# Copying the first transposed x tiles out of PSUM in smaller pieces, on two engines, with one warm-up matmul fewer

## The chip, the cores and the metric

The kernel runs on one core of one Trainium2 chip. The metric is the device time of one execution in microseconds (us). The times come with a profile of one execution, whose "span" is some 2 us shorter than the time. TensorE does the matmuls, VectorE and ScalarE copy and compute, GpSimd masks, and SyncE and ScalarE issue the DMAs of this stage. In the profile lines they are PE (with PEld for weight loads), DVE, ACT, POOL and SP.

## The reference, cut to what matters

```python
x = A_x                                             # 2048 x 512, bf16
g = _sigmoid((x * gate_w).sum(-1, keepdims=True))
a = _A_ref(x, ...)      # 4 segments of 512 tokens: causal attention of 32 heads plus a running memory, then @ wo
b = _B_ref(x, ...)      # (gelu(x @ w_gate) * (x @ w_up)) @ w_down
return g * a + (1 - g) * b
```

Every projection needs x with its features on the partitions, that is, transposed. The change touches only how the first segment of x gets there, in the first seven microseconds.

## The kernel before

The kernel is a fixed list of tasks for each engine (`ORDER`). An emitter works out the semaphore waits from the regions that the tasks read and write. The first segment of x is loaded untransposed in two halves of 256 tokens (u = 0, 1). TensorE transposes each half in 128 x 128 blocks into PSUM, and copies bring it to `xT[0]`. The other segments come through transposing DMAs.

```python
    for i in range(12):                                   # warm-ups ("fillers"): the product is never read
        gw = Grp(banks)
        n = 384 if i in (6, 9) else 512
        task(f"warm{i}", PE, [... e.matmul(gw.f32()[:, 0:n], ones[:, 0:128], ones[:, 0:n], ...)])
    XB = XALL.bitcast(BF)
    for u in range(2):                                    # half of the tokens
        for i in range(2):                                # two of the four feature blocks
            src = XB[:, 1024 * (2 * u + i):1024 * (2 * u + i) + 512]...      # one PSUM bank each
            key = ("X", 2 * u + i)
            task(f"x0t{i}_{u}", PE, [... e.transpose(...) for k in range(2) for a in range(2)])   # 4 transposes
            S.add(Task(f"x0ev{i}_{u}", {ACT: ..., DVE: [... e.tensor_copy(dst, src) ...]}))       # 512 columns
```

The heads of the orders; `K0_t.j` is matmul j of K tile t in the first segment. K matmuls 0 and 1 need feature blocks 0 and 1 of the first tokens, K matmuls 2 and 3 need blocks 2 and 3.

```python
"pe":  "warm0 ... warm9 x0t0_0 x0t1_0 warm10 warm11 K0_0.0 K0_1.0 K0_2.0 K0_3.0 K0_0.1 ... x0t0_1 x0t1_1 K0_0.2 ..."
"dve": "x0ev0_0 x0ev1_0 x0ev0_1 K0_1ev ..."
"act": "w_wk0 w_wk1 w_wq0 w_wq1 tload x0ev1_1 K0_0even ..."
```

The softmax here doesn't subtract the row's maximum and nothing guards it: scores larger than these inputs give would overflow.

## Time and profile before

| | before |
|---|---|
| time, median of the first 3 runs | 268.13 us (267.79 to 268.9) |
| span of the profiled execution | 265.8 us |
| TensorE busy | 261.9 us, 99% |
| first transpose, first K matmul (start) | 4.49, 5.40 us |

How to read it: TensorE is busy end to end, so anything that only shortens another engine's work cannot show. The stage to look at is the head. The distance from the first transpose to the first K matmul is the measure used throughout, because it does not contain the moment at which x arrives.

### The profile page before, as it was taken

What the parts mean: (1) busy time and instruction counts of PE and PEld (TensorE: products, weight loads), DVE (VectorE), ACT (ScalarE), POOL (GpSimd) and SP (SyncE); (2) the same over time, 40 slices, a digit from 0 to 9 for tenths busy, and PEclk for the clock granted to TensorE, in tenths of its full rate; (3) what the DMA queues carried; (4) which work ended last, traced back from release to release, by engine and by line L of the source; (5) the groups of instructions that cost most, each with busy time, mean ns of one, the idle gap of its engine ahead of it and who ended that gap; (6) DMA issues with size and microseconds to landing.
All of it is one profiled execution on the core that took longest, in us unless ns stands there. A gap on an engine that the chain in (4) does not pass through costs nothing.

```text
span 265.8 us, 7150 instructions
## 1 busy us (share of the span) xinstructions
PE 261.9 (99%) x3022; PEld 118.9 (45%) x3022; DVE 198.1 (75%) x389; ACT 210.1 (79%) x186; POOL 105.5 (40%) x256
## 2 busy tenths in 40 slices
PE   8999999999999999999999999999999999999995
PEld 4644354444444435444444444443444444343452
DVE  1798869988988588986767968898685847694651
ACT  2699998999998898898967888867876886767712
POOL 8204777453101358173830162354173071436310
PEclk9999999999999999999999999999999999999999
DMA  6952323518520433200001333200000031300102
GB/s 219 334 162 42 63 81 71 151 40 295 151 76 0 99 66 80 80 0 2 2 0 23 97 83 77 86 2 22 2 2 0 2 75 31 78 25 0 42 0 79
DMA packets 32751, 18.22 MB, mean 69 GB/s; under 512 B 20560, under 2 KB 32720, under 8 KB 32720
## 3 DMA queue, kind: packets, MB, share of 16 engines
q1 hardware_dynamic: 31632, 16.73, 23.5%
q10 hardware_dynamic: 1088, 1.05, 1.1%
q8 instruction: 23, 0.38, 0.6%
q14 instruction: 8, 0.07, 0.1%
HBM read 9.84 MB, written 2.10 MB: 45 GB/s over the span
## 4 chain that ended last, share of the span: by engine, by line
PE 98%; ACT 1%; issue 0%; ACTq 0%
PE psW L498 76%; PE psXALL L859 9%; PE psW L909 6%; PE psXALL L498 3%; PE psW L583 2%; PE psW L917 1%; PE psW L825 1%; ACT pt L866 1%; PE psXALL L591 0%; ACT ost L1038 0%; ACTq L394 0%
## 5 line engine op out<-in xcount | busy, mean ns | idle before, releaser
L866 ACT ACTIVATE pt<-psXALL 128x2048 bf16<-128x2048 f32 x64 | 120.1, 1877 | 25.2 <-PE psXALL L859 20.1
L870 POOL TENSOR_SCALAR_AFFINE_SELECT pt<-pt 128x256 bf16<-128x256 bf16 x128 | 57.3, 456 | 106.4 <-ACT pt L866 101.8
L498 PE MATMUL psW<-xT,wu 128*128 128x512 bf16 x224 | 56.3, 380 | 0.0
L498 PE MATMUL psW<-xT,wg 128*128 128x512 bf16 x224 | 54.2, 380 | 0.0
L498 PE MATMUL psW<-wd,hT 128*128 128x512 bf16 x210 | 53.5, 380 | 0.0
L1009 DVE TENSOR_TENSOR hT<-psW,hT 128x512 bf16<-128x512 f32 x56 | 37.2, 685 | 18.6 <-PE psW L498 18.2
L870 POOL TENSOR_SCALAR_AFFINE_SELECT ptl<-ptl 128x512 bf16<-128x512 bf16 x32 | 23.0, 720 | 33.4 <-ACT ptl L866 31.8
L924 DVE STREAM_TRANSPOSE tb<-psW 128x512 f32<-128x512 f32 x32 | 21.5, 699 | 14.0 <-PE psW L917 14.0
L498 PEld LDWEIGHTS psW<-xT,wg 128*128 128x128 bf16 x224 | 20.4, 98 | 24.3 <-issue 1.5
L498 PEld LDWEIGHTS psW<-xT,wu 128*128 128x128 bf16 x224 | 20.2, 98 | 24.4 <-issue 2.7
L498 PEld LDWEIGHTS psW<-wd,hT 128*128 128x128 bf16 x210 | 19.2, 98 | 22.8 <-issue 2.1
L859 PE MATMUL psXALL<-qT,kpad 32*128 32x320 bf16 (+3 forms) x512 | 25.4, 273 | 0.2 <-ACT pt L866 0.2
L993 ACT ACTIVATE hT<-psW 128x512 bf16<-128x512 f32 x28 | 15.4, 599 | 8.0 <-PE psW L498 8.0
L859 PEld LDWEIGHTS psXALL<-qT,kpad 32*128 32x128 bf16 x512 | 7.6, 92 | 25.8 <-ACT pt L866 16.1
L909 PE MATMUL psW<-pt,vaug 128*17 128x192 bf16 (+3 forms) x512 | 18.8, 273 | 0.0
L866 ACT ACTIVATE ptl<-psXALL 128x2048 bf16<-128x2048 f32 x8 | 15.0, 1877 | 3.7 <-PE psXALL L859 3.7
L498 PE MATMUL psW<-xT,wk 128*128 128x512 bf16 (+1 forms) x80 | 17.8, 337 | 0.0
L498 PE MATMUL psW<-wv,xT 128*128 128x512 bf16 x64 | 17.3, 381 | 0.0
L498 PE MATMUL psW<-wo,oT 128*128 128x512 bf16 x60 | 16.4, 380 | 0.0
L768 POOL COPY exsT<-exs 32x4 f32<-32x4 f32 x64 | 13.4, 210 | 7.2 <-ACT exs L759 3.5
L909 PEld LDWEIGHTS psW<-pt,vaug 128*17 128x17 bf16 x512 | 10.2, 90 | 8.8 <-issue 2.8
L498 PE MATMUL psW<-xT,wq 128*128 128x512 bf16 x48 | 12.8, 380 | 0.0
(101 smaller groups left out, 308.0 us busy)
## 6 DMA issues: line engine op xcount, KB each, us to landing
out_dram<-ost SPq DMA_DIRECT2D x15, 128.0 KB, 1.7
wg<-in_B_w_gate_dram SPq DMA_DIRECT2D x2, 896.0 KB, 6.8
wu<-in_B_w_up_dram SPq DMA_DIRECT2D x2, 896.0 KB, 6.0
wd<-in_B_w_down_dram SPq DMA_DIRECT2D x2, 896.0 KB, 5.8
phkt<-in_A_x_dram SPq DMA_DIRECT2D x3, 512.0 KB, 4.3
vlow<-vaug SPq DMA_DIRECT2D x8, 136.0 KB, 2.7
wk<-in_A_wk_dram ACTq DMA_DIRECT2D x2, 256.0 KB, 4.4
hT<-in_A_x_dram SPq DMA_DIRECT2D x2, 256.0 KB, 4.0
```

The costliest lines, as they stand in the source:

```text
L498: return Instr(lambda e: e.matmul(view(), lhsT, rhs, start=first, stop=last), reads=reads, writes=[fkey if fkey is not None else g.key], e ...
L583: task(f"warm{i}", PE, [Instr(lambda e, gw=gw, n=n: e.matmul(gw.f32()[:, 0:n], ones[:, 0:128], ones[:, 0:n], start=True, stop=True), [], [ ...
L768: cross = task(f"exsT{s}", POOL, [Instr(lambda e, g=g, c=c: e.tensor_copy(exsT[sl][32 * g:32 * g + 32, c:16:4], exs[32 * c:32 * c + 32, s4 ...
L825: Instr(lambda e, t=t, kt=kt, c=c: e.matmul(gm.f32()[32 * c:32 * c + 32, 34 * t:34 * t + 34].rearrange("p (j e) -> p j e", e=17), phkt[:, ...
L859: instrs.append(Instr(lambda e, g=g, lhs=lhs, rhs=rhs, c0=c0, ncol=ncol: e.matmul(X[g][:, c0:c0 + ncol], lhs(32 * g), rhs(32 * g), start=T ...
L866: prev_exp[0] = exp_task(s, f"exp{s}_{t}{name}", [Instr(lambda e: e.activation(dst[:], XALL[:, :].rearrange("p (g c) -> p g c", g=4), ACTF ...
L870: task(f"msk{s}_{t}{name}", POOL, [Instr(lambda e, view=view, pat=pat, base=base: e.affine_select(out=view, in_=view, compare_op=ALU.is_ge ...
L909: instrs.append(Instr(lambda e, t=t, q=q, kb=kb, slot=slot, c0=c0: e.matmul(gp.f32()[32 * q:32 * q + 17, 128 * kb + 64:512], Vaug[sl][:, k ...
L917: instrs.append(Instr(lambda e, t=t, q=q, kb=kb, c0=c0: e.matmul(gp.f32()[32 * q:32 * q + 17, 128 * kb:128 * kb + 64], Vlow[j][:, kb, 4 * ...
L924: task(f"pvt{s}_{t}_{j}", DVE, [Instr(lambda e: e.transpose(Tb[:, j, :], gp.f32()[:, :]), [gp.key], [("Tb", j)], dve_t(512))], grp=gp)
L993: lambda e, g=g, ft=ft, s=s: e.activation(hT[s % 2][:, ft, :], g.f32()[:, :], ACTF.Gelu_apprx_tanh),
L1009: task(f"Um{s}_{ft}", DVE, [Instr(lambda e, g=g, ft=ft: e.tensor_tensor(hT[sl][:, ft, :], g.f32()[:, :], hT[sl][:, ft, :], ALU.mult), [g.k ...
```

## The change

The intent is to start the first K matmul earlier. The first copy is cut into two of 256 columns, so the first K matmuls wait for half as much. The copy of feature blocks 2 and 3 of the first tokens goes to ScalarE, which is idle there. One filler behind the transposes is dropped and the other shortened to 384 columns.

```diff
-    for i in range(12):
+    for i in range(11):
-        n = 384 if i in (6, 9) else 512
+        n = 384 if i in (6, 9, 10) else 512
...
-    for u in range(2):
-        for i in range(2):
-            src = XB[:, 1024 * (2 * u + i):1024 * (2 * u + i) + 512].rearrange("p (k c) -> p k c", c=256)
-            key = ("X", 2 * u + i)
+    for nm, u, k0, nk, c0 in (("0a", 0, 0, 1, 0), ("0b", 0, 1, 1, 1024), ("1", 0, 2, 2, 2048),
+                              ("0", 1, 0, 2, 3072), ("1", 1, 2, 2, 512)):
+        src = XB[:, c0:c0 + 256 * nk].rearrange("p (k c) -> p k c", c=256)
+        key = ("x0ps", c0)
...   (the same transposes and copies, nk blocks at a time)
 "pe":
-  ... x0t0_0 x0t1_0 warm10 warm11 K0_0.0 ...
+  ... x0t0a_0 x0t0b_0 x0t1_0 warm10 K0_0.0 ...
 "act":
-  ... tload x0ev1_1 ...
+  ... tload x0ev1_0 x0ev1_1 ...
 "dve":
-  x0ev0_0 x0ev1_0 x0ev0_1 ...
+  x0ev0a_0 x0ev0b_0 x0ev0_1 ...
```

## The prediction

> **What bounds the kernel now.** I read the page first: the engine table, then the chain of work that ended last. After that I read the first 16 us in the timeline, one engine at a time, because everything the diff touches lies there. Last came the DMA issues of the first microseconds, to see which arrival could take back what the change gives. From the page:
>
> ```profile
> PE 261.9 (99%) x3022; PEld 118.9 (45%) x3022; DVE 198.1 (75%) x389; ACT 210.1 (79%) x186; POOL 105.5 (40%) x256
> ...
> PE 98%; ACT 1%; issue 0%; ACTq 0%
> ```
>
> The span is 265.8 us and the matmul row is busy for 261.9. Of the 3.9 us left over, 0.84 lie before the first warm-up and about 2.8 after the last matmul (the chain in order of time has its last matmuls at 261.94 for 0.99 us, so 265.8 - 262.93). That leaves under 0.3 us of holes in between. Inside, the matmuls run at their full rate: the chain has one piece of 78 matmuls in 16.63 us, 0.213 us each for 512 columns. So TensorE is the bound from end to end, and only work taken out of its stream, or a hole closed in it, can shorten the kernel. Granted clock is full in the windows I asked for. The head of the stream, timeline of TensorE:
>
> ```profile
> 0.84 3.62 PE L583 MATMUL psW<-const-bfloat16-1.0 128*128 128x512 bf16 x10 [0.84 <-PEq L1164]
> 4.49 0.62 PE L591 MATMUL psXALL<-ident,hT 128*128 128x128 bf16 x8
> 4.94 0.60 PE L583 MATMUL psW<-const-bfloat16-1.0 128*128 128x512 bf16 x2
> 5.40 1.05 PE L498 MATMUL psW<-xT,wk 128*128 128x256 bf16 x8
> 6.29 0.61 PE L591 MATMUL psXALL<-ident,hT 128*128 128x128 bf16 x8
> 6.73 2.46 PE L498 MATMUL psW<-xT,wk 128*128 128x256 bf16 x21
> ```
>
> Columns are start, length, engine, line, operation, operands and count. Ten warm-up matmuls fill the wait for the first half of x. Eight transposes follow, then two more warm-ups, then the first eight K matmuls. L583 is pure filler: its product is never read. Between 4.94 and 5.40 the tensor engine does nothing of use. What it waits for there is in the next two views, VectorE and the weight loads:
>
> ```profile
> 4.92 0.75 DVE L599 COPY xT<-psXALL 128x512 bf16<-128x512 bf16 x2 [4.92 <-PE psXALL L591]
> ...
> 5.40 0.11 PEld L498 LDWEIGHTS psW<-xT,wk 128*128 128x128 bf16 x2 [0.36 <-DVE xT L599]
> ```
>
> The two copies are 0.42 us each (a narrow window shows the second starting at 5.26, before the first is through). The first runs from 4.92 to 5.34, and the first K weight load starts 0.06 later. The second filler starts at 5.16 and needs 0.22, so it ends its streaming at about 5.38. Copy and filler therefore end together; taking away only one would give 0.02 to 0.03 us at most.
>
> **What the Trainium skill says.** "VectorE: DVE Perf Modes", section "The TRN2 errata", gives PSUM to SBUF copies 120 + FD/Accel cycles at 0.96 GHz, and its tier table allows at most 2x for a PSUM operand. For 512 bf16 columns at 2x that is 392 ns; the trace has 414 to 425, so 2x holds and the fixed part is some 158 ns (425 - 267). "ScalarE: Activation LUTs", section "What ACT_TABLE_LOAD costs", gives an ACTIVATE with immediates 186 ns + 0.833 ns per column, 613 ns for 512; the one such copy in the trace took 597 ns. "TensorE: Matmul & The Clock Gate", Part 1, gives warm matmuls N/2.4 + 2.5 ns apart: 216, 162 and 109 ns for 512, 384 and 256 columns. The trace agrees where it can be seen: the fillers are 0.22 apart and the eight K matmuls take 5.40 to 6.29, 0.111 each. "PSUM — Partial Sum Buffer", section "PSUM bank collisions raise a hardware error", says that two engines must not touch one bank at once. The new layout respects this: the two quarter pieces and ScalarE's half lie in three banks, and the piece that reuses the first bank comes over 1 us later.
>
> **The change part by part.**
>
> Smaller first pieces. The first copy now waits for two transposes instead of four. Four started at 4.49 to 4.66, 0.055 apart, and the copy began at 4.92; two save 2 x 0.055 = 0.11, so it begins at 4.81. For 256 columns at 2x I take 158 + 133 = 0.29 us, so it ends at 5.10, and with the same 0.06 hop the K weight load may start at 5.16. The second quarter starts about 0.21 behind the first and ends near 5.31. It is needed only by the fifth K matmul, at 5.16 + 4 x 0.11 = 5.60.
>
> One filler less, and a shorter one. The transposes end where they did, so the one filler left begins at 4.94, and with 384 columns it streams until 5.10. That is just below the 5.16 of the copy. The copy binds, and a hole of about 0.06 us stays.
>
> The second half to ScalarE. It waits for the eighth transpose (start 4.89, end 5.11), begins at about 5.15 and ends at 5.75. Its readers are K matmuls after the second group of transposes, that is after 5.16 + 0.89 + 0.44 = 6.49. It is hidden by 0.7 us. ScalarE has nothing else to do then: the table load and its dummy ended at 4.40, and its next item was at 6.93. VectorE loses one 0.42 us copy that nothing waited for.
>
> Sum: the first K matmul moves from 5.40 to 5.16, 0.24 us. The rest of the stream is the same work back to back, so the end moves by 0.24 less what an arrival takes back. No instruction on the path becomes longer.
>
> **The rivals.**
>
> First, arrivals that do not move. TensorE is now close behind its data. The loads of the first half of this stage, with the median time from issue to landing:
>
> ```profile
> wk<-in_A_wk_dram ACTq DMA_DIRECT2D x1, 256.0 KB, 4.8
> hT<-in_A_x_dram SPq DMA_DIRECT2D x1, 256.0 KB, 4.5
> ...
> wq<-in_A_wq_dram ACTq DMA_DIRECT2D x2, 256.0 KB, 6.6
> ```
>
> The second half of x was issued near 1.27 to 1.33 and lands at about 5.8; its transposes would start at 6.05 instead of 6.29. The second half of wk lands at about 6.1 and is needed at 6.49. The second half of wq was issued at 2.37 and took 7.1 (the longest of its tile), so it lands at 9.47. Its first reader is the fifth Q matmul, at 9.03 + 4 x 0.215 = 9.89 before and 9.65 after, with its weight load a little earlier. That margin is 0.1 to 0.2 us, so 0 to 0.1 us of the gain may be lost there, and all of it in a run in which this load is late. Against a bigger loss: only one wait of TensorE for a DMA is in the whole table of waits (0.5 us, for the first half of x), and later loads have half a microsecond or more (second half of wg: issued at 12.13, 5.2 to landing, so 17.3, used at 18.05). Time if this eats everything: 268.1.
>
> Second, the clock. One filler fewer could let the tensor clock fall back, and a colder start costs half the rate while it lasts. The skill's clock page, Part 1, puts the idle time needed at about 3.4 us; the hole left here is 0.06 us, and TensorE has been active since 0.84. If it did happen, some microseconds at half rate would add 1 to 2 us (269 to 270). I give that 3 in 100.
>
> Third, knock-on effects: fewer instructions on TensorE's queue and another rotation of PSUM banks from here on could open or close small holes later, where TensorE has nearly none to close. I allow 0.1 to 0.2 us of either sign. A large gain is ruled out by the table above: the whole head up to the first K matmul is 5.4 us, 2% of the span, and most of it is waiting for x.
>
> **Range and chances.** 268.13 - 0.24, less some 0.04 for the wq arrival, is 267.9 us. The effect is smaller than the scatter: the three runs before lie between 267.79 and 268.9. A median of three scatters by perhaps 0.4 us, estimated from these, which is most of my range: 267.3 to 268.6. To leave the 2% band the time would have to be under 262.8 or over 273.5. Same has 0.985.
>
> **What would show each step right or wrong.** In the changed profile: VectorE's first copy 128x256, 0.27 to 0.30 us, starting near 4.81 if x lands as before; the first K matmul at about 5.16 (or 0.67 us after the first transpose, against 0.91 now); one 384-column filler; a ScalarE copy of 128x512 near 5.15 of 0.60 us that no one waits for; second transposes near 6.05; and the first exp 0.2 us earlier than its 15.16. A wait of the weight loads for hT, wk or wq in the list of waits would show the first rival; a granted clock below full after 5 us would show the second. The prediction is wrong if the first K matmul moves by 0.24 and the end does not, or if the 256-column copy is not shorter by 0.13 us.

## The result

| | before | after |
|---|---|---|
| time, median of 6 runs each | 268.23 us (267.79 to 268.9) | 267.54 us (267.1 to 268.4) |
| span of the profiled execution | 265.8 us | 265.4 us |
| first transpose, first K matmul | 4.49, 5.40 | 4.34, 5.01 |
| distance between the two | 0.91 us | 0.67 us |
| start of ScalarE's last instruction | 263.04 us | 262.64 us |

The ratio is 0.9977, 95% interval 0.9954 to 1.0. A ratio is the mean time of one kernel's fast runs over that of the other's in the same rounds, so it is not quite the ratio of the two medians. The class is "same", as forecast.

The page of the changed kernel, engine table and chain:

```profile
PE 261.5 (99%) x3021; PEld 119.0 (45%) x3021; DVE 197.8 (75%) x389; ACT 210.6 (79%) x187; POOL 105.4 (40%) x256
...
PE 98%; ACT 1%; issue 0%; ACTq 0%
```

One TensorE instruction fewer, one ScalarE instruction more, and the same bound. The timeline of TensorE at the head (start, length, then what):

```profile
0.84 3.55 PE L583 MATMUL psW<-const-bfloat16-1.0 128*128 128x512 bf16 x10 [0.84 <-PEq L1164]
4.34 0.62 PE L591 MATMUL psXALL<-ident,hT 128*128 128x128 bf16 x8
4.80 0.33 PE L583 MATMUL psW<-const-bfloat16-1.0 128*128 128x384 bf16 x1
5.01 1.05 PE L498 MATMUL psW<-xT,wk 128*128 128x256 bf16 x8
5.90 0.61 PE L591 MATMUL psXALL<-ident,hT 128*128 128x128 bf16 x8
6.34 2.46 PE L498 MATMUL psW<-xT,wk 128*128 128x256 bf16 x21
```

From the same timeline of the changed kernel, VectorE's first copies, ScalarE's copy and the first K weight load:

```profile
4.66 0.49 DVE L599 COPY xT<-psXALL 128x256 bf16<-128x256 bf16 x2 [4.66 <-PE psXALL L591]
...
5.00 0.60 ACT L598 ACTIVATE xT<-psXALL 128x512 bf16<-128x512 bf16 x1 [0.59 <-PE psXALL L591]
...
5.01 0.77 PEld L498 LDWEIGHTS psW<-xT,wk 128*128 128x128 bf16 x8 [0.17 <-DVE xT L599]
```

The weight load still waits for VectorE, but for a shorter copy and from an earlier start. The end of the chain in order of time, kernel before and then changed kernel:

```profile
263.04 0.58 ACT ost L1038
```

```profile
262.64 0.58 ACT ost L1038
```

The end came 0.40 us earlier. Of this, 0.24 us is the shorter distance from first transpose to first K matmul (0.91 - 0.67). Another 0.15 us is the first transpose itself, at 4.34 instead of 4.49; nothing in the change comes before it. From the first K matmul to ScalarE's last instruction both executions took the same, 257.64 and 257.63 us. So one profile of each supports 0.24 us for the change, and the medians say 0.69. The experiments ask which of the two it is, and which part of the change does it.

### The profile page after: what moved, and what is told of

The parts are those of the page before. It is cut to its first block, busy times and chain, and to the rows that moved or that the text cites. A ratio compares the mean times of both kernels' runs of the same rounds, so it can differ in the third digit from the quotient of the medians.

```text
span 265.4 us, 7149 instructions
## 1 busy us (share of the span) xinstructions
PE 261.5 (99%) x3021; PEld 119.0 (45%) x3021; DVE 197.8 (75%) x389; ACT 210.6 (79%) x187; POOL 105.4 (40%) x256
## 4 chain that ended last, share of the span: by engine, by line
PE 98%; ACT 1%; issue 0%; ACTq 0%
PE psW L498 76%; PE psXALL L859 9%; PE psW L909 6%; PE psXALL L498 3%; PE psW L917 1%; PE psW L583 1%; PE psW L825 1%; ACT pt L866 1%; PE psXALL L591 0%; ACT ost L1038 0%; ACTq L394 0%
```

## The experiments

Two theories stood at the start. First: the change moves the first K matmul by 0.24 us, TensorE's stream behind it is rigid, and the rest of the measured difference is scatter of single executions. Rival: the change is worth the whole 0.4 to 0.7 us. Below that was a question of parts: copy, filler or ScalarE's relief.

All outputs are right. The table holds what the timelines show. "Fillers" is the length of the ten warm-ups ahead of the transposes. "Rest" is from the first K matmul to the start of ScalarE's last instruction. All are in us.

| run | fillers | first transpose | first K matmul | distance | last ScalarE instruction | rest |
|---|---|---|---|---|---|---|
| before (first profile) | 3.62 | 4.49 | 5.40 | 0.91 | 263.04 | 257.64 |
| after (first profile) | 3.55 | 4.34 | 5.01 | 0.67 | 262.64 | 257.63 |
| before_rep | 4.21 | 4.85 | 6.55 | 1.70 | 264.26 | 257.71 |
| after_rep | 4.21 | 4.85 | 5.58 | 0.73 | 263.35 | 257.77 |
| after_rep2 | 4.21 | 4.89 | 5.92 | 1.03 | 263.68 | 257.76 |
| pieces_only | 3.74 | 4.64 | 5.53 | 0.89 | 263.14 | 257.61 |
| filler_only | 4.21 | 4.85 | 5.83 | 0.98 | 263.46 | 257.63 |
| half_on_dve | 3.83 | 4.51 | 5.17 | 0.66 | 262.80 | 257.63 |
| no_filler | 3.90 | 4.58 | 5.25 | 0.67 | 262.87 | 257.62 |
| eight_more | 4.21 | 4.85 | 7.73 | 2.88 | 265.38 | 257.65 |
| cold_before | none | 4.64 | 6.33 | 1.69 | 264.76 | 258.43 |
| cold_after | none | 4.20 | 5.35 | 1.15 | 263.81 | 258.46 |
| x_split9 | 3.89 (nine) | 4.53 | 5.45 | 0.92 | 265.39 | 259.94 |
| cold_no_filler | none | 4.86 | 5.69 | 0.83 | 266.18 | 260.49 |

### Both kernels again, unchanged (before_rep, after_rep, after_rep2)

No edit.

> The kernel before, unchanged, for the scatter. Theory (the head gains 0.24 us, the rest of the 0.4 us by which the two profiled spans differ is the moment at which x arrived): from the first transpose to the first K matmul 0.91 us again, first transpose anywhere from 4.3 to 4.7, time within 0.2% of the kernel before. Rival (the whole 0.4 us is the change): the first transpose again near 4.49 and the span near 265.8, within 0.1.

> The changed kernel, unchanged. Theory: from the first transpose to the first K matmul 0.67 us again whenever x arrives, ratio near 0.9985 with an interval about 0.1 or 0.2% wide. Rival (all of the measured 0.23% is the change): ratio again 0.9977 or less, and the first transpose again near 4.34.

> The changed kernel once more, to add to its times. Theory (gain of 0.24 us with an early clock release, about 0.5 with a late one): ratio 0.998 to 0.999; first transpose to first K matmul 0.66 to 0.75 if the clock is up by then, up to 1.17 if not; from the first K matmul to the start of ScalarE's last instruction 257.6 to 257.8 us. Rival (a gain of 0.6 us as first measured): ratio 0.9977 again and more than 0.3 us found behind the first K matmul.

Measured: before_rep 268.54 us, ratio 1.0006 (0.9976 to 1.0036). after_rep 268.02 us, ratio 0.9997 (0.9963 to 1.003). after_rep2 268.63 us, ratio 1.0012 (0.998 to 1.0044), against 268.10 us of the kernel before in its rounds. The first 0.9977 did not come back, so the rival's "all of the 0.23% is the change" has no support. The three ratios of the changed kernel against the one before lie on both sides of 1, and their intervals hold 0.999. The 95% intervals are some 0.3% to either side, wider than the effect, so the times cannot decide between 0.24 us and nothing.

Several of my expectations missed. Before_rep was to show a distance of 0.91 us and a first transpose by 4.7, and showed 1.70 and 4.85. After_rep was to show 0.67 us and an interval of 0.1 to 0.2%, and showed 0.73 and 0.67%. After_rep2 was to have a ratio of 0.998 to 0.999, and had 1.0012. The TensorE timeline of before_rep:

```profile
0.84 4.21 PE L583 MATMUL psW<-const-bfloat16-1.0 128*128 128x512 bf16 x10 [0.84 <-PEq L1164]
4.85 1.06 PE L591 MATMUL psXALL<-ident,hT 128*128 128x128 bf16 x8
5.70 1.06 PE L583 MATMUL psW<-const-bfloat16-1.0 128*128 128x512 bf16 x2
6.55 1.12 PE L498 MATMUL psW<-xT,wk 128*128 128x256 bf16 x8
```

In this execution the clock of TensorE was still at half rate. The eight transposes are 0.106 us apart (4.85 to 5.70) instead of 0.055, and the fillers 0.43 instead of 0.22. Ten fillers took 4.21 us where the first profile had 3.62. The moment at which the clock goes up is thus not fixed. It can move the first transpose, which cannot start before the fillers end: in filler_only x had landed at 4.28, and the first transpose came at 4.85. Here x itself landed only at 4.80, so x and the fillers tie. And it changes the distance that this change works on. This is a third theory, which I formed here: the change gains more in an execution whose clock goes up late. The two repeats of the changed kernel fit it. In after_rep the first two gaps between transposes are 0.11 and 0.07 us and the rest 0.055 (distance 0.73). In after_rep2 all but the first are about 0.106 (distance 1.03).

After_rep shows one more thing, in the timeline of the weight loads:

```profile
10.19 0.33 PEld L498 LDWEIGHTS psXALL<-xT,wq 128*128 128x128 bf16 x3 [0.46 <-DMA wq<-in_A_wq_dram]
```

The second half of wq landed at 10.15, when its first reader was due at 10.07. That matmul started 0.34 us after the one before it instead of 0.22, so some 0.12 us of the gain was lost. This is the first rival of the prediction.

### One half of the change at a time (pieces_only, filler_only)

```diff
 pieces_only, against the changed kernel
-    for i in range(11):                              +    for i in range(12):
-        n = 384 if i in (6, 9, 10) else 512          +        n = 384 if i in (6, 9) else 512
-  ... x0t1_0 warm10 K0_0.0 ...                       +  ... x0t1_0 warm10 warm11 K0_0.0 ...
 filler_only, against the kernel before
-    for i in range(12):                              +    for i in range(11):
-        n = 384 if i in (6, 9) else 512              +        n = 384 if i in (6, 9, 10) else 512
-  ... x0t1_0 warm10 warm11 K0_0.0 ...                +  ... x0t1_0 warm10 K0_0.0 ...
```

> The changed kernel with both 512-column fillers after the transposes put back. Theory (copy and filler ended together, both had to go): first transpose to first K matmul 0.88 to 0.90 us, so only 0.02 to 0.03 of the 0.24 gained, with PE and not VectorE as what the weight load is behind; time like the kernel before within 0.1%. Rival (the smaller copy alone makes the gain): 0.67 to 0.70 us.

> The kernel before with the one shorter filler, copies as before. Theory: VectorE's 512-column copy still ends 0.85 us after the first transpose, so first transpose to first K matmul stays 0.89 to 0.91 us and the tensor engine stands idle some 0.27 us before it; time like the kernel before within 0.1%. Rival (the filler alone makes the gain): 0.63 to 0.70 us.

With the smaller copies but both fillers the distance was 0.89 us, against 0.91 with neither part and 0.67 with both. The first K weight load of pieces_only, and then that of filler_only:

```profile
5.31 0.97 PEld L498 LDWEIGHTS psW<-xT,wk 128*128 128x128 bf16 x8
```

```profile
5.82 0.77 PEld L498 LDWEIGHTS psW<-xT,wk 128*128 128x128 bf16 x8 [0.41 <-DVE xT L599]
```

In pieces_only the weights were loaded at 5.31, 0.22 ahead of their matmul at 5.53, and no wait for VectorE is named: the fillers held TensorE. In filler_only the weight load sat idle for 0.41 us until VectorE's copy. Its distance, 0.98, is over the expected 0.91 because its clock went up late (fillers 4.21; the first two gaps between transposes are 0.11 and 0.07 us instead of 0.07 and 0.06). Neither half alone gains more than 0.02 us. The times (268.11 and 268.75 us, ratios 1.0005 for both) say nothing at this size.

### The second half back on VectorE (half_on_dve)

```diff
 "act":  -  ... tload x0ev1_0 x0ev1_1 ...        +  ... tload x0ev1_1 ...
 "dve":  -  x0ev0a_0 x0ev0b_0 x0ev0_1 ...        +  x0ev0a_0 x0ev0b_0 x0ev1_0 x0ev0_1 ...
```

> The changed kernel with the copy of the second half of the first transposes given back to VectorE, behind its two quarter copies. Theory (that copy was hidden before and is hidden after): first transpose to first K matmul 0.66 to 0.68 us with a warm clock, no wait of a K matmul for it, and the end where it was. Rival (ScalarE's relief of VectorE is part of the gain): the distance to the ninth K matmul or to VectorE's first cast of kT grows by 0.1 us or more.

Distance 0.66 us, rest 257.63. The second transposes followed the first K matmul by 0.88 us (5.17 to 6.05), against 0.89 in the changed kernel, and VectorE's first cast of kT by 2.73 (7.90), against 2.74. The time was 267.81 us, ratio 0.9975 (0.995 to 0.9999). Moving that copy to ScalarE is worth nothing here: it was hidden before and is hidden after.

### No filler, and eight more (no_filler, eight_more)

```diff
 no_filler    -  ... x0t1_0 warm10 K0_0.0 ...     +  ... x0t1_0 K0_0.0 ...
 eight_more   -  ... x0t1_0 warm10 K0_0.0 ...     +  ... x0t1_0 warm10 warm11 ... warm18 K0_0.0 ...
```

> The changed kernel without any filler between transposes and first K matmul. Theory (with the clock warm VectorE's first copy is what binds): first transpose to first K matmul 0.66 to 0.68 us, unchanged; if the profile falls in an execution whose clock is released late, the eight transposes take 0.107 us each and the distance is 0.85 to 0.9. Rival (the filler still binds): 0.60 or less with a warm clock. Time equal to the changed kernel within what can be seen.

> The changed kernel with eight more 512-column fillers between the transposes and the first K matmul. Theory (TensorE's stream is rigid: whatever moves the first K matmul moves the end by the same): first transpose to first K matmul 0.67 - 0.05 (the hole the fillers close) + 8 x 0.216 = 2.35 us with a warm clock; from the first K matmul to the start of ScalarE's last instruction 257.6 to 257.8 us as in every profile so far; time 1.7 us (0.6%) over the changed kernel, ratio to the kernel before 1.0045 to 1.006. Rival (slack later in the kernel swallows delays, or gains, of the head): 257.0 or less from first K matmul to the last ScalarE instruction, ratio under 1.002.

Without the last filler the distance stays 0.67 us, so with a raised clock VectorE's quarter copy is what binds in the changed kernel, as predicted. The time was 267.95 us, ratio 0.9982 (0.9954 to 1.0011).

With eight fillers more the first K matmul came at 7.73, and everything behind it moved along: the rest was 257.65 us. The time was 269.7 us, ratio 1.0045 (1.0018 to 1.0072), the low edge of what was expected. The distance of 2.88 instead of 2.35 is again a late clock: its transposes are at half rate (4.85 to 5.70), and the first filler behind them is slow too (0.28 us for 384 columns). The rival, slack later in the kernel, is refuted by the rest column. It is the same to 0.16 us in ten runs whose first K matmul lies anywhere between 5.01 and 7.73. The three largest have a reason in their traces: the wait for wq in after_rep, a first K matmul at half rate in before_rep (0.08 us), and in after_rep2 a wait for a copy of VectorE at 41.6 us (0.12 us).

### The change at half clock (cold_before, cold_after)

```diff
-  "pe": warm0 ... warm9 x0t0...                  +  "pe": x0t0...          (the ten leading fillers dropped in both)
```

> The kernel before without its first ten fillers, so that TensorE's clock is still at half rate at its first transposes in every execution. Theory (the change gains more in an execution whose clock is released late): eight transposes of 0.107 and two fillers of 0.427 us put the first K matmul 1.70 us after the first transpose, as in the repeat of the kernel before; from there on some matmuls at half rate, so the end 2 to 4 us later than with fillers. Rival (the clock has nothing to do with it): 0.9 us.

> The changed kernel without its first ten fillers. Theory: 8 x 0.107 + 0.32 for the 384-column filler gives 1.17 us from first transpose to first K matmul, 0.53 less than its partner without the change, because now the filler and not VectorE's copy binds; the two quarter copies end well before. Rival (the gain is 0.24 at any clock): 1.46 us. In time its ratio to the kernel before should be about 0.002 below that of its partner.

The heads of both, TensorE's timeline, cold_before and then cold_after:

```profile
4.64 1.04 PE L591 MATMUL psXALL<-ident,hT 128*128 128x128 bf16 x8 [4.64 <-DMA hT<-in_A_x_dram]
5.47 1.06 PE L583 MATMUL psW<-const-bfloat16-1.0 128*128 128x512 bf16 x2
6.33 1.85 PE L498 MATMUL psW<-xT,wk 128*128 128x256 bf16 x8
```

```profile
4.20 1.03 PE L591 MATMUL psXALL<-ident,hT 128*128 128x128 bf16 x8 [4.20 <-DMA hT<-in_A_x_dram]
5.03 0.52 PE L583 MATMUL psW<-const-bfloat16-1.0 128*128 128x384 bf16 x1
5.35 1.87 PE L498 MATMUL psW<-xT,wk 128*128 128x256 bf16 x8
```

The distances are 1.69 and 1.15 us, a gain of 0.54 where 0.53 was expected and the rival had 0.24. The transposes and the filler alone fill the distance in cold_after, so at half clock the filler binds and not the copy. The ratios to the kernel before were 1.0034 and 1.0014, and their difference of 0.002 is the expected size, though each interval is 0.003 to either side. The rest was longer by 0.8 us, because the first eight K matmuls ran at half rate too (0.21 apart). I had expected the end 2 to 4 us later; cold_before's last ScalarE instruction was 1.72 later than in the first profile of before, and 0.50 later than in before_rep.

x alone set the first transpose here, and it came at 4.64 and 4.20 with the same loads (and at 4.86 in the next run). So the arrival of x scatters by some 0.7 us.

### No filler at all (cold_no_filler)

```diff
-  "pe": warm0 ... warm9 x0t0a_0 x0t0b_0 x0t1_0 warm10 K0_0.0      +  "pe": x0t0a_0 x0t0b_0 x0t1_0 K0_0.0
```

> The changed kernel without any filler at all, so with a clock still at half rate at the first transposes. Theory: the eight transposes at 0.107 us are then all there is between, and the first K matmul follows the first transpose by 0.85 to 0.88 us, 0.29 less than with the 384-column filler at this clock (measured 1.15); VectorE's first copy would allow 0.78. Rival (VectorE's copy also binds at half rate): 1.0 us or more.

The distance was 0.83 us, near the expected 0.85 and far from the rival's 1.0. But the time was 270.58 us, ratio 1.0081 (1.0047 to 1.0115), and the rest grew to 260.49 us. Some 0.8 of that is cold K matmuls and about 0.2 the second transposes, also partly at half rate. Most of the remainder is one hole, in the timeline of TensorE:

```profile
36.04 0.27 PE L917 MATMUL psW<-ptl,vlow 128*17 128x64 bf16 x11
37.93 0.23 PE L917 MATMUL psW<-ptl,vlow 128*17 128x64 bf16 x5 [1.62 <-issue]
```

TensorE waits 1.62 us for nothing that the profile shows as a dependence, in the middle of a group of sixteen tiny matmuls. The DMA view shows a load on the instruction queue between 34 and 38 us here. In no_filler, which has no such hole, the corresponding load is between 30 and 34. The Trainium skill's page "Runtime: NRT & Kernel Launch", section "Instruction fetch mechanics", says that instructions come in blocks of 256 and that crossing a block is mostly hidden. A late block fits the hole, but that it was the cause is argued and not shown. It needs only 22 TensorE instructions fewer than the changed kernel. cold_after, with 20 fewer, has no such hole.

### Loading the first x faster (x_split9)

```diff
-  "sp":  x0_0 x0_1 ...                              +  "sp":  x0_0a x0_1 ...      (rows 0 to 127)
-  "act": w_wk0 w_wk1 ...                            +  "act": x0_0b w_wk0 w_wk1 ...   (rows 128 to 255)
-  "pe":  ... warm8 warm9 x0t0a_0 ... warm10 K0_0.0  +  "pe":  ... warm8 x0t0a_0 ... warm9 K0_0.0
```

> The changed kernel with the first 256 rows of x loaded by two DMAs of 128 rows, one on each issuing queue ahead of wk, and one filler fewer ahead of the transposes. Theory (the arrival of x sets the first transpose): it starts at 4.0 to 4.3 us where the changed kernel had 4.34 and 4.85, and the first K matmul about 0.2 us earlier, near 4.8, unless wk becomes the last to arrive. Rival (the same bytes have to come in any order): the weight load waits for the DMA of wk, and the first K matmul is no earlier than 5.0.

This was an attempt at something better than both kernels, and it failed: 269.92 us, ratio 1.0062 (1.0036 to 1.0088). In its timeline of TensorE, after the second transposes:

```profile
8.71 0.49 PE L498 MATMUL psW<-xT,wk 128*128 128x256 bf16 x3 [1.78 <-DMA wk<-in_A_wk_dram]
```

The halves of x landed sooner (2.6 us after issue for the quickest, against 3.5 in the changed kernel), but with a late clock the nine fillers still held the first transpose at 4.53. The second half of wk took up to 6.8 us from issue to landing, against 4.7, and TensorE stood idle for it. The fifth Q matmul then lost another 0.4 us to the second half of wq. The rival was right in kind: what is brought forward on these queues pushes something else back.

## Why the prediction was right or wrong

The time lies in the range (267.54 in 267.3 to 268.6), and "same" was right. As a test of the mechanism this says little, and luck has a part in it: the range is mostly scatter, and after_rep2, the same kernel at 268.63 us, would have fallen just outside. The test is the distance, forecast to go from 0.91 to 0.67 us, and it did. Step by step:

- **TensorE is the bound from end to end: right.** eight_more and the rest column show that the end follows the first K matmul one for one.
- **The first copy: right.** It was to start 0.32 us after the first transpose (4.81 - 4.49) and did (4.66 - 4.34). It was to take 0.29 us; the two copies of 256 columns took 0.28 and 0.29.
- **Copy and filler end together, so only both count: right.** pieces_only gained 0.02 us, filler_only nothing that can be seen, both together 0.24.
- **ScalarE's half is hidden: right.** It started 0.66 us after the first transpose, as predicted, took 0.60, and half_on_dve showed that it makes no difference.
- **A hole of 0.06 us stays and the copy binds: right with a raised clock.** no_filler left the distance at 0.67.
- **First rival, an arrival that does not move: right, in one repeat.** I took off 0.04 us for wq and allowed 0 to 0.1. In the first profile wq cost nothing: it landed at 9.27, and its matmul started on time at 9.50. In after_rep it took 0.12 us. x_split9 shows it larger: with wk later, TensorE waited 1.78 us.
- **Second rival, the clock: the wrong question.** I asked whether the clock falls back with one filler fewer, and gave it 3 in 100. No head shows it falling back. What I missed is that it goes up at a different moment in each execution. That moment can hold up the first transpose (by 0.2 us or more in five runs, see the next point) and it sets the size of the gain. The term mis-sized is the "sum" of 0.24 us: it holds for a clock that is up by then, and was 0.54 us with a clock at half rate (1.69 - 1.15). I also read "granted clock is full" from the windows view, which gave 1.00 over the first 4.46 us although most of the fillers there stood 0.43 us apart; the 0.22 that I quoted holds for the last ones. The spacing of the matmuls was the better witness.
- **"Most of it is waiting for x": only half so.** The first transpose waits for the later of two things, x and the end of the leading fillers. In six of the eleven runs with leading fillers it follows the landing of x by about 0.05 us, the two first profiles among them. In the other five (filler_only, half_on_dve, no_filler, eight_more, x_split9) x had landed 0.2 us or more before it, and the fillers were still running.
- **Third rival, small holes elsewhere: none in the first profile of the changed kernel.** After_rep2 has one of 0.12 us, within what I allowed. cold_no_filler shows a large one, 1.62 us, with more instructions removed.

**What stays open.** The first measurement had 0.69 us between the medians, the traces explain 0.24 to 0.54, and the repeats showed 0.9997 and 1.0012. The share of executions with a late clock among the timed ones is not known, because only one of each six was traced. The scatter of the times hides the rest. Taken together, the five ratios of kernels with the short head (the three of the changed kernel, no_filler and half_on_dve) have a mean of 0.9989, or 0.3 us: the size that the traces give, but each is uncertain by 0.3%, so the times agree with the gain and do not prove it.

## What to carry to other kernels

When an engine is held by two things that end together, shortening one of them gains nothing; look for the second one before building, and test each alone. A gain of a few tenths of a microsecond is settled by a distance within the trace, not by the time of the whole kernel. Fillers that keep a clock up also delay the work behind them, and in a stream with no slack even removing instructions can open a hole far away.

## What the Trainium skill lacked or had wrong

- "TensorE: Matmul & The Clock Gate", Part 1, has the clock go up around 4 us into sustained matmuls, give or take 0.5 us from run to run (it also warns that the count of slow matmuls varies). Here the fillers start at 0.84 us in every run that has them. In the first profile of the changed kernel they stood 0.22 us apart from 3.63 on, 2.8 us after the first. In before_rep the matmuls were at half rate until the first K matmul at 6.55, 5.7 us after the first. That is a spread of nearly 3 us. The page's advice to warm up for 4 us is thus not enough in every execution.
- The same page, Part 4, says that full rate does not engage for transposes. Here eight transposes stood 0.055 us apart with a raised clock (4.49 to 4.89 for the first and the eighth) and 0.106 with a low one (before_rep), as 256-column K matmuls went from 0.11 to 0.21.
- "Runtime: NRT & Kernel Launch", section "Instruction fetch mechanics", calls the cost of a block boundary mostly hidden. If the hole of 1.62 us in cold_no_filler is such a boundary (argued, not shown), a stretch of many tiny matmuls does not hide it.
- No page that I read says how much the landing of the last store varies. The last output transfer of 96 KB landed 1.6 us after issue in most profiles, and 3.0 and 2.9 us in after_rep and filler_only. Their spans were 267.5 us for that reason, with ScalarE's last instruction no later than 263.5.
